# New durations, landing times and priorities for the list planner of a fused attention and expert kernel

## The chip, the core and the metric

The kernel runs on one core of a Trainium2 chip. The metric is the time of one execution in device microseconds, lower is better. The kernel before takes 679.66 us, the median of three runs (678.16 to 679.78).

A core has engines that each work through a queue of instructions in order and wait for each other by semaphores: PE (matrix products into PSUM banks), DVE and ACT (elementwise work), POOL (here mostly the issue of loads) and SP (here the issue of stores).

## The reference

```python
# block attention: a band of +-16 positions, and summaries of blocks of 32
a = softmax(concat(where(mask_l, scale * q @ k.T, -1e9), scale * q @ k_sum.T + log(32)))
x = (a @ concat(v, v_sum)).transpose(0, 2, 1, 3).reshape(3072, 512)
# a dense mixture of experts; P comes from 8 rounds of row and column scaling
P = exp(x @ w_gate - max)
for _ in range(8):
    P /= P.sum(1); P /= P.sum(0); P *= N / E
for e in range(8):
    out += P[:, e:e+1] * (maximum(x @ w1[e], 0) @ w2[e])      # w1[e]: 512 x 1024, w2[e]: 1024 x 512
```

## The kernel before

A first part (to about 164 us of the profiled execution) computes the attention, the gate and expert 0 by ordinary products, and, in a "bridge", the first block of expert 1 beside the eight rounds of scaling. Then comes the repeating part: experts 1 to 7 with both products of each expert done by Winograd's form of Strassen's method (7 block products in place of 8, for more additions). The repeating part is what the change touches.

Each expert `e` is cut into three blocks of columns `j`, and each block into two duos `u` (functions `duo` and `plan_duo`) for the first product and four pairs `c` (functions `pair` and `plan_pair`) for the second.

- A **duo** has two sides, K = 0 and 1. Each side has the PE products `p1` to `p7`, each of two 512 column matmuls (line 990). Between them stand the ACT copies `seed` (line 1091), `c5` (line 1099), `c2` (line 1106), the ACT relus `r11` and `r21` (line 217), and the DVE additions with relu `c12` and `c22` (line 940). `p6` needs `seed`, `p3` needs `c5`, `p7` needs `c2`, `p4` needs `c22`. There is one buffer each for `c5` and for `c2`, so the `c5` copy of one side waits until `c22` of the side before has read the buffer. After both sides come four DVE additions of 1024 columns, `s1` to `s4` (lines 934 and 937).
- From block 2 of expert 1 on, the `p1` of both sides are themselves done by the method: seven single 256 column matmuls `m1` to `m7` (line 1040) with ACT copies `sd` and `c5s` and the DVE additions `j1` (before `m3` and `m7`) and `j2` (before `m4`), which are two of the uses of line 937. There are 38 such split duos among 42.
- A **pair** has the products `q1` to `q7`, each of four 256 column matmuls (line 996), into two banks x and y. ACT makes `c1` and `v6`, DVE makes `v5` (needed by `q6`) and then four accumulations `y0` to `y3` into the output (line 1215). In the last block the pairs c = 1 and 3 use other banks and end in `z0` to `z4`, `x0` and `x1` instead. In expert 1, ACT also scales the output (`scale_a`, `scale_b`, line 1163).
- Beside these, DVE forms the sums of the next expert's weights: `w1_sum` (256 columns), `w2_sum` (1024 columns, four per expert, the first called T1 here) and `wa_sum` (128 columns). POOL issues the loads: `load_w1` (two of 128 KB) and `load_w2` (one of 1 MB).

PSUM has two banks each for the tags ab, g, x and y. A `p1` or `p5` opens an ab bank and so waits until the last user of the old one (`r11` or `c12`) is done.

The order of all this on each engine is not written by hand. `Plan.order` (line 60) is a list planner that runs while the kernel is built: it keeps a clock for each engine, takes for each engine the unit that can start first (within 0.02 us, the one of lowest priority number), lets it last the duration that the code gives (`us`, line 1274), and adds small lags from engine to engine. The instructions are emitted in the order in which they are taken, so every engine's queue is fixed at build time; durations and priorities decide nothing else. Priorities of the repeating part come from the table `PR` (line 1410) plus a base that grows by 100 per duo. For a load the planner assumes an issue time, 0.8 us, a landing time (the fourth argument of `load`) and 0.4 us; units that need the loaded weights start after that.

Of the kernel before, what the change touches and what calls it, by code (L numbers as in the profile page):

```python
# [140 lines left out]
def kernel(  # L141
# [12 lines left out]
    B, H, S, D = q.shape  # L154
# [765 lines left out]
    if True:  # L920
# [232 lines left out]
        def pair(e, j, c, spare=False, tail=False, c1_at=None):  # L1153
# [111 lines left out]
            def x1():  # L1265
# [5 lines left out]
            return {f.__name__: f for f in (scale_a, scale_b, q1, c1, q5, v5, q6, v6, q2, q7, q3, q4, y0, y1, y2, y3, fin, ahead,  # L1271
                                            z3, z2, z0, z4, x0, x1)}

        us = dict(m=0.1092, p=0.4316, q=0.4368, seed=0.49, c5=0.49, c2=0.49, r=0.49, c12=0.607, c22=0.607, s=0.6,
                  c1=0.275, v6=0.275, v5=0.34, y=0.665, half=0.275, join=0.34, w1=0.205, w2=0.6, wa=0.14, x=0.6,
                  xa=0.2, sc=0.62, part=0.34)
        LAGS = {"ACT": 0.06, "DVE": 0.04}

        def put(eng, cost, fn, deps, prio, opens=(), uses=()):
# [121 lines left out]
        for u in course:  # L1401
# [6 lines left out]
        plan.more({"x": 2, "y": 2, "c1": 1, "m5": 1})  # L1408

        PR = {  # L1410
# [8 lines left out]
        }  # L1419
        QO = dict(q1=0, c1=.1, q5=.2, v5=.3, q6=.4, v6=.5, q2=.6, q4=.7, q7=.8, q3=.9)  # L1420
        duos = [(e, j, u) for e in range(1, E) for j in range(NJ) for u in range(2)]
        pairs = {}

        def weights(e, i, deps):
            load(("w1", e, i), lambda: load_w1(e, i), 0.85, 1.3, deps)

        def w_sums(e, i, prio, old=()):
            for n in range(4):
# [26 lines left out]
        def plan_pair(e, j, c, prio):  # L1455
            last_block = e == E - 1 and j == NJ - 1
            spare = last_block and c % 2 == 1
            c1_at = None
            if spare:
                c1_at = lambda: fast.tile([128, 512], FP32, tag=("c2", "c5")[c // 2], name="c1t", bufs=1)[:, 0:DH]  # L1460
            f, d = pair(e, j, c, spare, last_block, c1_at), {}
            src = [made[e, j, 0], made[e, j, 1]]

            def of(*names):
                return [x[n] for x in src for n in names]

            def op(name, eng, cost, deps, opens=(), uses=(), p=None):
                d[name] = put(eng, cost, f[name], [d[y] if isinstance(y, str) else y for y in deps],
                              prio + (QO[name] if p is None else p), opens=opens, uses=uses)

            bx, by = (Buffer(t) for t in (("ab", "g") if spare else ("x", "y")))
            k1 = Buffer("c1")
            c1s = [] if spare else [k1]
            m = us["q"]
            op("q1", "PE", m, of("r110", "r111") + [U["w2", e]] + ([src[1]["c121"], src[1]["r211"]] if spare else []),
               [bx, by])
            op("c1", "ACT", us["c1"], ["q1"] + ([src[1]["c121"], src[1]["c221"]] if spare else []), c1s, [bx])
            op("q5", "PE", m, ["q1", W2[e, 0]] + of("s1"), (), [bx])
            op("v5", "DVE", us["v5"], ["q5", "c1"], (), [bx, by] + c1s)
            op("q6", "PE", m, ["v5", W2[e, 1]] + of("s2"), (), [by])  # L1480
            op("v6", "ACT", us["v6"], ["q6"], (), [by])
            op("q2", "PE", m, ["c1"] + of("r210", "r211"), (), [bx])
            op("q4", "PE", m, ["v5", W2[e, 3]] + of("c220", "c221"), (), [bx])
            op("q7", "PE", m, ["v6", W2[e, 2]] + of("s3"), (), [by])
            op("q3", "PE", m, ["v6"] + of("s4"), (), [by])
            old = []
            if e == 1:
                op("scale_b", "ACT", us["sc"], [], p=PR["sc"])
                op("scale_a", "ACT", us["sc"], [], p=PR["sc"])
                old = ["scale_a", "scale_b"]  # L1490
            if spare:
                op("ahead", "POOL", 0.75, [pairs[e - 1, j, c][y] for y in ("y1", "y2")], p=0)
                op("z3", "ACT", us["half"], ["q3"], (), [by], p=1)
                op("z2", "DVE", us["v5"], ["q7", "ahead"], (), [by], p=1)
                op("z0", "DVE", us["v5"], ["z2"], (), [by], p=1.1)
                op("z4", "POOL", 0.75, ["z3"], p=1)
                op("x0", "DVE", us["v5"], ["q2", "z4"], (), [bx], p=2)
                op("x1", "DVE", us["v5"], ["q4", "z0"], (), [bx], p=2.1)
            else:
                op("y0", "DVE", us["v5"], ["q2"] + old[:1], (), [bx], p=PR["yd"])  # L1500
                op("y1", "DVE", us["v5"], ["q4"] + old[1:], (), [bx], p=PR["yd"] + .1)
                op("y2", "DVE", us["v5"], ["q7"] + old[1:], (), [by], p=PR["yd"] + 2)
                op("y3", "DVE", us["v5"], ["q3", "y0"] + old[:1], (), [by], p=PR["yd"] + 2.1)
                if e == E - 1:
                    op("fin", "POOL" if last_block else "DVE", 0.75 if last_block else us["part"], ["y1", "y2"],
                       p=PR["yd"] + 1)
            pairs[e, j, c] = d

        def feed(n):
            base = 10000.0 + 100.0 * n  # L1510
            if n < len(duos):
                e, j, u = duos[n]
                k = 2 * j + u
                if n == 2:
                    for m in range(4):
                        X[2, m] = put("DVE", us["x"], lambda m=m: x_sum(2, m), [X.get((2, m - 1))], base + 30 + 15 * m)
                    xa_sums(2, base + 100)
                split = None
                if (e, j) >= (1, 2):
                    split = [U["wa", e, u, m] for m in range(4)] + [XA[j, m] for m in range(4)]  # L1520
                free = pair_users(*duos[n - 4][:2]) if n >= 4 else []

                def prio(name):
                    if name in ("s1", "s3", "s2", "s4"):
                        return base + PR["S"] + 0.1 * ("s1", "s3", "s2", "s4").index(name)
                    return base + PR[{"p10": "m1", "p11": "m4"}.get(name, name)]

                made[e, j, u] = plan_duo(e, j, u, prio, split, [made[duos[n - 1]]["p51"]], free,
                                         {(2 * u + h, m): WT[e, 2 * u + h, m] for h in range(2) for m in range(4)},
                                         [X[j, m] for m in range(4)])  # L1530
                if n == 3:
                    p1s = ("p10", "p11")
                    for v in range(2):
                        wa_sums(1, v, base + 30 + 10 * v, users(1, 0, v, p1s) + users(1, 1, v, p1s))
                    for i in range(2):
                        xa_sums(i, base + 150 + 100 * i, users(1, i, 0, p1s) + users(1, i, 1, p1s))
                if e + 1 < E:
                    w = base + PR["w"]
                    if k == 2:
                        load(("w2", e + 1), lambda: load_w2(e + 1), 0.9, 5.0, pair_users(e - 1, 2))  # L1540
                        weights(e + 1, 0, users(e - 1, 2, 1))
                    if k == 3:
                        w2_sums(e + 1, (0, 1), w + 20, pair_users(e - 1, 2))
                        w_sums(e + 1, 0, w, users(e - 1, 2, 1))
                    if k == 4:
                        w2_sums(e + 1, (2, 3), w + 20)
                        weights(e + 1, 1, users(e, 2, 0))
                        weights(e + 1, 2, users(e, 2, 0))
                    if k == 5:
                        w_sums(e + 1, 1, w - 100, users(e, 2, 0))  # L1550
                        wa_sums(e + 1, 0, w - 90, users(e - 1, 2, 1))
                        w_sums(e + 1, 2, w, users(e, 2, 0))
                        weights(e + 1, 3, users(e, 2, 1))
                        w_sums(e + 1, 3, w + 10, users(e, 2, 1))
                        wa_sums(e + 1, 1, w + 20, users(e, 2, 0))
            m = n - 2
            if m < len(duos):
                e, j = duos[m][:2]
                for c in range(2):
                    plan_pair(e, j, 2 * (m % 2) + c, base + PR[f"q{c}"])  # L1560
# [41 lines left out]
```

## Time and profile before

| | us |
| --- | --- |
| median of three runs | 679.66 |
| the profiled execution's own time | 679.68 |
| its span, first to last instruction | 677.7 |
| PE busy | 664.1 |
| DVE busy | 573.5 |
| ACT busy | 420.8 |
| POOL busy | 133.4 |

A row of the timeline gives the start, the duration, the engine, the line, the operation, the tiles (out, then in), the shape and the count of merged instructions, and in brackets the idle time before it and what ended it. A matmul's recorded duration is longer than the time until the next one starts, since they are pipelined; the distance between two starts is what counts for PE. The same holds, less so, for DVE and ACT. A row of stretches gives, after the stretch, the busy time and the number of instructions of each engine, the granted PE clock (1.00 is full), and the use of the DMA engines. Where it is asked for one line only, it counts that line's instructions.

### The profile page before, as it was taken

To read this page: it belongs to the slowest core of one execution; us is meant where nothing else is said; L and a number is where in the kernel's file an instruction comes from. 1 tells how busy PE (TensorE), PEld (TensorE's weight loads), DVE (VectorE), ACT (ScalarE), POOL (GpSimd) and SP (SyncE) were. 2 spreads that over 40 slices of the span, in tenths; PEclk is the share of its full clock that TensorE was granted. 3 is DMA by queue.
4 is the path that set the end of the run, shared out by engine and by line. 5 is a ranking of instruction groups with operands and counts; after the bars stand their busy time and mean duration, and the time that the engine had idled before them with its cause. 6 is when DMAs were issued, how large, how long until landed. Compare 5 with 4: busy or idle time off the path is not lost.

```text
span 677.7 us, 13610 instructions
## 1 busy us (share of the span) xinstructions
PE 664.1 (98%) x5191; PEld 446.7 (66%) x5191; DVE 573.5 (85%) x1447; ACT 420.8 (62%) x858; POOL 133.4 (20%) x179
## 2 busy tenths in 40 slices
PE   8999999999899999999999999999999999999996
PEld 4666655555466676676776766767667667676675
DVE  7889998677789789887988888978988798888795
ACT  6777775566795655665656656565566565665642
POOL 8699404222011010201010010101020101000001
PEclk9999999999899999999999999999999999999999
DMA  9999939401313041310531051304131053101215
GB/s 164 183 149 146 141 72 93 70 1 24 55 17 32 1 66 14 38 11 3 77 32 17 1 78 13 36 1 67 13 36 13 5 75 32 17 1 45 81 63 186
DMA packets 124032, 36.74 MB, mean 54 GB/s; under 512 B 110144, under 2 KB 121152, under 8 KB 123968
## 3 DMA queue, kind: packets, MB, share of 16 engines
q0 software_dynamic: 104128, 25.93, 40.7%
q1 hardware_dynamic: 18880, 9.22, 6.2%
q8 instruction: 40, 0.66, 0.4%
q10 hardware_dynamic: 960, 0.74, 0.3%
q14 instruction: 24, 0.20, 0.1%
HBM read 52.45 MB, written 6.29 MB: 87 GB/s over the span
## 4 chain that ended last, share of the span: by engine, by line
PE 70%; DVE 23%; issue 2%; DMA 2%; ACT 2%; DVEq 0%; ACTq 0%
PE px L996 16%; PE pab L990 12%; PE pg L990 12%; PE py L996 10%; DVE out_acc L1215 6%; PE yps L236 5%; PE hps L226 5%; PE pab L1040 3%; DVE hf L940 3%; DVE hf L934 3%; DVE ws L934 2%; DVE pab L937 1%; DMA w<-in_moe_w_dram 1%; DVE xs L552 1%; DVE hf L937 1%
## 5 line engine op out<-in xcount | busy, mean ns | idle before, releaser
L996 PEld LDWEIGHTS <-hf 128*128 128x128 f16 x2352 | 230.1, 98 | 86.2 <-issue 3.4
L996 PE MATMUL px<-w,hf 128*128 128x256 f16 x656 | 97.9, 273 | 0.0
L996 PE MATMUL px<-ws,hf 128*128 128x256 f16 x656 | 96.1, 274 | 0.0
L996 PE MATMUL py<-w,hf 128*128 128x256 f16 x656 | 93.4, 272 | 0.7 <-DVE out_acc L1215 0.4
L217 ACT ACTIVATE hf<-pab 128x512 f16<-128x512 f32 x84 | 50.2, 599 | 68.2 <-PE pab L990 50.4
L940 DVE CUSTOM_DVE_ANT_0 hf<-pg,c 128x512 f16<-128x512 f32 x84 | 57.6, 686 | 33.7 <-ACT c L1099 30.2
L934 DVE TENSOR_TENSOR hf<-hf 128x1024 f16<-128x1024 f16 x126 | 85.7, 681 | 0.4 <-ACT hf L217 0.3
L202 POOL DMA_DIRECT2D w<-in_moe_w_dram x56 | 41.7, 755 | 215.6 <-PE pg L990 180.5
L1215 DVE SCALAR_TENSOR_TENSOR out_acc<-py,P_sb,out_acc 128x256 f32<-128x256 f32 x164 | 75.2, 474 | 2.7 <-PE py L996 2.6
L1215 DVE SCALAR_TENSOR_TENSOR out_acc<-px,P_sb,out_acc 128x256 f32<-128x256 f32 x164 | 74.4, 474 | 2.1 <-PE px L996 2.1
L940 DVE CUSTOM_DVE_ANT_0 hf<-pab,c 128x512 f16<-128x512 f32 x84 | 57.7, 686 | 21.5 <-PE pab L990 17.7
L990 PEld LDWEIGHTS <-w 128*128 128x128 f16 x520 | 50.8, 98 | 33.2 <-issue 3.6
L1099 ACT COPY c<-pab 128x512 f32<-128x512 f32 x84 | 49.2, 586 | 37.2 <-DVE hf L940 19.6
L1091 ACT COPY pg<-pab 128x512 f32<-128x512 f32 x84 | 48.0, 573 | 33.2 <-PE pab L1040 33.0
L990 PEld LDWEIGHTS <-ws 128*128 128x128 f16 x504 | 49.1, 98 | 28.0 <-issue 7.1
L217 ACT ACTIVATE hf<-pg 128x512 f16<-128x512 f32 x84 | 50.6, 602 | 14.8 <-PE pg L990 12.5
L990 PE MATMUL pab<-xT,w 128*128 128x512 f16 x184 | 54.8, 382 | 0.0
L990 PE MATMUL pg<-xTs,w 128*128 128x512 f16 x168 | 49.9, 378 | 2.9 <-DVE hf L940 2.9
L990 PE MATMUL pab<-xT,ws 128*128 128x512 f16 x168 | 50.0, 379 | 0.6
L990 PE MATMUL pg<-xT,w 128*128 128x512 f16 x168 | 50.4, 382 | 0.0
L1106 ACT COPY c<-pg 128x512 f32<-128x512 f32 x84 | 49.4, 588 | 1.6 <-PE pg L990 1.5
L990 PE MATMUL pg<-xTs,ws 128*128 128x512 f16 x168 | 49.7, 378 | 0.0
(168 smaller groups left out, 1094.7 us busy)
## 6 DMA issues: line engine op xcount, KB each, us to landing
w<-in_moe_w_dram POOLq DMA_DIRECT2D x8, 1024.0 KB, 9.0
w<-in_moe_w_dram POOLq DMA_DIRECT2D x56, 128.0 KB, 3.6
out_dram<-out_acc SPq DMA_DIRECT2D x20, 256.0 KB, 2.1
vx<-in_v_dram POOLq DMA_DIRECT2D x16, 192.0 KB, 6.0
qst<-in_q_dram POOLq DMA_DIRECT2D x31, 96.0 KB, 5.5
kst<-in_k_dram POOLq DMA_DIRECT2D x24, 96.0 KB, 5.4
w<-in_moe_w_dram POOLq DMA_DIRECT2D x2, 512.0 KB, 8.7
Ve<-vx SPq DMA_DIRECT2D x48, 10.2 KB, 4.3
```

The costliest lines, as they stand in the source:

```text
L202: nc.gpsimd.dma_start(out=t[:, :, h, :], in_=moe_w1[e].rearrange("(dk p) f -> p dk f", p=128)[:, :, f:f + 128])
L217: nc.scalar.activation(out=out, in_=in_, func=AF.Relu, bias=0.0, scale=1.0)
L226: nc.tensor.matmul(hp[:, 0:n], lhsT=w1s[e][:, dk, 128 * f:128 * (f + 1)], rhs=xT[:, dk, t0:t0 + n], start=(dk == 0), stop=(dk == KD - 1))
L236: nc.tensor.matmul(yp[:], lhsT=h[:, f, c * 128:(c + 1) * 128], rhs=w2s[e][:, f, :], start=(f == 0), stop=(f == KF - 1))
L934: nc.vector.tensor_tensor(out=out, in0=in0, in1=in1, op=ALU.subtract)
L940: nc.vector._custom_dve(TENSOR_ADD_SAT, out=out, in0=in0, in1=in1, s0=FLT_MAX, s1=0.0)
L990: nc.tensor.matmul(bank[:], lhsT=w[:, dk, :], rhs=x[:, dk, :], start=start and dk == 0, stop=dk == KH - 1, skip_group_check=True)
L996: nc.tensor.matmul(bank, lhsT=a(f)[:, 128 * c:128 * (c + 1)], rhs=w[:, f, :], start=start and f == 0, stop=f == FH - 1, skip_group_check=True)
L1091: nc.scalar.copy(out=B["g" + K][:], in_=B["a" + K][:])
L1099: nc.scalar.copy(out=B["c5" + K][:], in_=B["b" + K][:])
L1106: nc.scalar.copy(out=B["c2" + K][:], in_=B["g" + K][:])
L1215: nc.vector.scalar_tensor_tensor(out=acc, in0=at(src), scalar=P_sb[:, t, e:e + 1], in1=acc, op0=ALU.mult, op1=ALU.add)
```

## The change

Numbers of the planner are changed, and with them the order in which the units come out. No unit is added or removed.

```diff
-        us = dict(m=0.1092, p=0.4316, q=0.4368, seed=0.49, c5=0.49, c2=0.49, r=0.49, c12=0.607, c22=0.607, s=0.6,
-                  c1=0.275, v6=0.275, v5=0.34, y=0.665, half=0.275, join=0.34, w1=0.205, w2=0.6, wa=0.14, x=0.6,
-                  xa=0.2, sc=0.62, part=0.34)
+        us = dict(m=0.1092, p=0.4316, q=0.4368, seed=0.55, c5=0.5, c2=0.49, r=0.49, c12=0.607, c22=0.607, s=0.6,
+                  c1=0.34, v6=0.28, v5=0.35, y=0.395, half=0.275, join=0.335, w1=0.205, w2=0.6, wa=0.14, x=0.6,
+                  xa=0.2, sc=0.63, part=0.34)
...
-            "m1": -147.7, "sd": -402.0, "m5": -279.9, "c5s": 449.5, "m2": -40.2, "m6": -290.7,
...
+            "m1": -361.0, "sd": -416.8, "m5": -89.0, "c5s": 512.2, "m2": -93.3, "m6": -289.5,
...
-            load(("w1", e, i), lambda: load_w1(e, i), 0.85, 1.3, deps)
+            load(("w1", e, i), lambda: load_w1(e, i), 0.85, 2.5, deps)
...
-                op("y0", "DVE", us["v5"], ["q2"] + old[:1], (), [bx], p=PR["yd"])
-                op("y1", "DVE", us["v5"], ["q4"] + old[1:], (), [bx], p=PR["yd"] + .1)
-                op("y2", "DVE", us["v5"], ["q7"] + old[1:], (), [by], p=PR["yd"] + 2)
-                op("y3", "DVE", us["v5"], ["q3", "y0"] + old[:1], (), [by], p=PR["yd"] + 2.1)
+                op("y0", "DVE", us["y"], ["q2"] + old[:1], (), [bx], p=PR["yd"])
+                op("y1", "DVE", us["y"], ["q4"] + old[1:], (), [bx], p=PR["yd"] + .1)
+                op("y2", "DVE", us["y"], ["q7"] + old[1:], (), [by], p=PR["yd"] + 2)
+                op("y3", "DVE", us["y"], ["q3", "y0"] + old[:1], (), [by], p=PR["yd"] + 2.1)
...
-                        load(("w2", e + 1), lambda: load_w2(e + 1), 0.9, 5.0, pair_users(e - 1, 2))
+                        load(("w2", e + 1), lambda: load_w2(e + 1), 0.9, 8.0, pair_users(e - 1, 2))
```

So the accumulations `y0` to `y3`, and `z0`, `z2`, `x0`, `x1` of the last block in the same way, are planned with 0.395 us in place of 0.34; `seed`, `c5`, `c1`, `v6` and `v5` last a little longer in the plan; a `load_w2` lands 3.0 us later in the plan and a `load_w1` 1.2 us later; and all 43 numbers of `PR` but one are new.

More of the change, by code (lines that the diff above doesn't have):

```diff
@@ L1493, in plan_pair @@
                 op("z3", "ACT", us["half"], ["q3"], (), [by], p=1)
-                op("z2", "DVE", us["v5"], ["q7", "ahead"], (), [by], p=1)
-                op("z0", "DVE", us["v5"], ["z2"], (), [by], p=1.1)
+                op("z2", "DVE", us["y"], ["q7", "ahead"], (), [by], p=1)
+                op("z0", "DVE", us["y"], ["z2"], (), [by], p=1.1)
                 op("z4", "POOL", 0.75, ["z3"], p=1)
-                op("x0", "DVE", us["v5"], ["q2", "z4"], (), [bx], p=2)
-                op("x1", "DVE", us["v5"], ["q4", "z0"], (), [bx], p=2.1)
-            else:
-                op("y0", "DVE", us["v5"], ["q2"] + old[:1], (), [bx], p=PR["yd"])
-                op("y1", "DVE", us["v5"], ["q4"] + old[1:], (), [bx], p=PR["yd"] + .1)
-                op("y2", "DVE", us["v5"], ["q7"] + old[1:], (), [by], p=PR["yd"] + 2)
-                op("y3", "DVE", us["v5"], ["q3", "y0"] + old[:1], (), [by], p=PR["yd"] + 2.1)
+                op("x0", "DVE", us["y"], ["q2", "z4"], (), [bx], p=2)
+                op("x1", "DVE", us["y"], ["q4", "z0"], (), [bx], p=2.1)
+            else:
+                op("y0", "DVE", us["y"], ["q2"] + old[:1], (), [bx], p=PR["yd"])
+                op("y1", "DVE", us["y"], ["q4"] + old[1:], (), [bx], p=PR["yd"] + .1)
+                op("y2", "DVE", us["y"], ["q7"] + old[1:], (), [by], p=PR["yd"] + 2)
+                op("y3", "DVE", us["y"], ["q3", "y0"] + old[:1], (), [by], p=PR["yd"] + 2.1)
                 if e == E - 1:
```

14 rows, old and new, of the table PR are left out of this document.

## Prediction

> **What bounds the kernel now.** I read the page first, then the waits, then PE's timeline by the distance between starts, since the recorded length of a matmul hides small waits.
>
> ```profile
> span 677.7 us, 13610 instructions
> ...
> w<-in_moe_w_dram POOLq DMA_DIRECT2D x8, 1024.0 KB, 9.0
> ```
>
> ```profile
> 164.10 1.03 PE L990 MATMUL pab<-xT,w 128*128 128x512 f16 x4
> 164.96 1.04 PE L996 MATMUL px<-w,hf 128*128 128x256 f16 x8
> 165.83 1.03 PE L990 MATMUL pg<-xTs,ws 128*128 128x512 f16 x4
> 166.70 1.03 PE L990 MATMUL pab<-xT,w 128*128 128x512 f16 x4
> 167.56 0.59 PE L990 MATMUL pg<-xT,w 128*128 128x512 f16 x2
> ```
>
> Eight matmuls of 512 columns start within 165.83 to 167.56: 0.216 us each. Eight of 256 take 164.96 to 165.83: 0.109. So a `p` costs 0.43 and a `q` 0.44 when nothing waits. Here PE runs without a gap. Counting matmuls in two stretches, by lines 990, 996 and 1040, shows how much it loses elsewhere:
>
> ```profile
> 182.00:657.97 475.97, 253.73 (x934) 90.86 (x933) 1.00 0.23 32
> 407.22:480.69 73.47, 39.31 (x145) 14.02 (x145) 1.00 0.25 30
> ```
>
> ```profile
> 182.00:657.97 475.97, 294.59 (x2174) 212.13 (x2173) 1.00 0.23 32
> 407.22:480.69 73.47, 45.59 (x338) 32.77 (x336) 1.00 0.25 30
> ```
>
> ```profile
> 182.00:657.97 475.97, 62.20 (x266) 25.94 (x266) 1.00 0.23 32
> 407.22:480.69 73.47, 9.95 (x42) 4.09 (x42) 1.00 0.25 30
> ```
>
> Long stretch: 934 x 0.216 + 2440 x 0.109 = 467.7 of 475.97, a loss of 8.3 us. One expert (407.22 to 480.69, the same point of the next one): 144 x 0.216 + 378 x 0.109 = 72.3 of 73.5, a loss of 1.15 (145 and 338 reach over the edge). Experts 2 to 6 repeat it: 5.8 of the 8.3; the other 2.5 lie where expert 1 passes into 2, and in expert 7. So PE's work bounds the repeating part, and an order can win back only such losses, and one larger one:
>
> ```profile
> 171.47 0.60 PE L996 MATMUL px<-w,hf 128*128 128x256 f16 x4
> 174.95 0.59 PE L990 MATMUL pg<-xTs,w 128*128 128x512 f16 x2 [2.88 <-DVE hf L940]
> ```
>
> ```profile
> 169.75 0.43 DVE L937 TENSOR_TENSOR py<-px,c 128x256 f32<-128x256 f32 x1 [0.62 <-ACT c L1187]
> 173.60 0.69 DVE L934 TENSOR_TENSOR ws<-w 128x1024 f16<-128x1024 f16 x1 [3.42 <-DMA w<-in_moe_w_dram]
> 174.21 0.68 DVE L940 CUSTOM_DVE_ANT_0 hf<-pg,c 128x512 f16<-128x512 f32 x1
> ```
>
> ```profile
> 164.56 0.94 POOL L213 DMA_DIRECT2D w<-in_moe_w_dram  x1 [1.41 <-PE yps L236]
> ```
>
> ```profile
> 175.00:180.00 5.00, 4.99 (x19) 2.45 (x19) 4.57 (x11) 3.95 (x7) 0.00 (x0) 0.66 0.00 0
> ```
>
> The 1 MB load of expert 2's `w2` is issued at 164.56 and lands 9.0 later, at 173.6. DVE has come to T1 of those weights at 170.2 and stands 3.42; `c22` is behind it in the queue, and PE's `p4` waits for `c22`. PE's four matmuls end their slot at 171.47 + 0.44 = 171.91, so it idles 3.04. Then the granted clock is 0.66 over the next 5.0 us: another 5.0 x 0.34 = 1.7. Together 4.7 us. (The Trainium skill, page "TensorE: Matmul & The Clock Gate", Part 1, says that PE goes to half clock after an idle window of about 3.4 us that runs freely; the trace agrees that some 3 us suffice.)
>
> **The change, part by part.** No instruction is added or removed, and up to the bridge the queues stand as before; only places in the order change.
>
> *The landing times.* The plan before expects `w2` 0.8 + 5.0 + 0.4 = 6.2 after its issue unit, the new one 9.2; the row says 9.0 from issue. In the new DVE order T1 stands behind `v5`, `c22`, `y0`, `c12` and the second `v5`, all of expert 1, block 1. I walk through that place from the 164.10 of `p1`.
>
> ```profile
> 164.78 1.07 ACT L1091 COPY pg<-pab 128x512 f32<-128x512 f32 x2
> 165.77 0.39 ACT L1187 COPY c<-px 128x256 f32<-128x256 f32 x1
> 166.03 0.74 ACT L1163 ACTIVATE out_acc<-out_acc,P_sb 128x512 f32<-128x512 f32 x1
> ```
>
> ACT's new order after the two seeds (end 165.85) is scale, `c2`, `c1`, `r11`, `r11`, scale, `c5`: `c2` can start at 166.6, and 0.6 + 0.4 + 0.6 + 0.6 + 0.7 + 0.6 put the end of `c5` at 170.1 (copies and relus of 512 columns at 0.6, the longest reading of the row of seeds). `c22` (0.68) then ends at 170.85, and `p4`, 15 products after 164.10 and so due at 170.6, loses 0.3. The second `v5` follows `q5`, the 17th product: DVE reaches T1 at about 172.4 and waits 1.2 for 173.6 instead of 3.4. T1 takes until 174.2, `c12` until 174.9; this frees the bank of the 24th product, a `p1` due at about 174.5: 0.4. With 0.1 each at `p3` and `p7`, behind ACT, PE loses 0.9. Bounds: 0.5, when ACT's ops take their shorter distance; 2.0, when `c22`, one op later than `c12`, also holds `p4`, and the first of these waits adds up. No wait comes near 3 us, so I take the clock as full. Gain 4.7 - 0.9 = 3.8 (2.7 to 4.2). The loads themselves are issued in the same order on POOL, and in the repeating experts no row has DVE waiting for a load: there the later landing costs nothing, hidden by a block of PE work.
>
> *The durations.* What is lost in a repeating expert shows in two kinds of places.
>
> ```profile
> 406.46 0.68 DVE L940 CUSTOM_DVE_ANT_0 hf<-pg,c 128x512 f16<-128x512 f32 x1
> ...
> 411.46 0.68 DVE L934 TENSOR_TENSOR hf<-hf 128x1024 f16<-128x1024 f16 x1
> 412.06 0.48 DVE L1215 SCALAR_TENSOR_TENSOR out_acc<-px,P_sb,out_acc 128x256 f32<-128x256 f32 x1
> 412.46 0.42 DVE L937 TENSOR_TENSOR pab<-pab,m 128x256 f32<-128x256 f32 x1
> ```
>
> ```profile
> 407.23 0.59 ACT L1099 COPY c<-pab 128x512 f32<-128x512 f32 x1 [0.66 <-DVE hf L940]
> ```
>
> ```profile
> 407.22 0.59 PE L990 MATMUL pg<-xTs,w 128*128 128x512 f16 x2
> 407.86 0.59 PE L990 MATMUL pab<-xT,ws 128*128 128x512 f16 x2
> ```
>
> ```profile
> 412.06 0.60 PE L996 MATMUL px<-w,hf 128*128 128x256 f16 x4
> 412.59 0.60 PE L996 MATMUL px<-ws,hf 128*128 128x256 f16 x4
> ```
>
> First: `c22` ends late on a full DVE (407.14), the `c5` copy waits for its buffer and ends at 407.82, and `p3` starts 0.64 after the product before it instead of 0.43: 0.21 lost, in two of an expert's duos. Second: `q4` starts at 412.59, 0.53 after `q2`, since `y0` on its bank stood behind an `s` until 412.06: 0.1 lost. The distance between starts says why: an `s` holds DVE 0.60 and a `y` 0.40, and the old plan had 0.34 for a `y`. With 48 of them per expert, 48 x 0.06 = 2.9 us of DVE work were not in the plan. The new one has 0.395.
>
> I then counted in both orders how much PE work stands between an op's trigger and the product that needs the op. From `p5` to `p3` (over `c5`) the least is 0.87 before and 1.31 after; it needs 0.16 (a matmul group's 0.59 less its 0.43) + 0.59 + some 0.1 of signals = 0.85 with a free ACT, so the new order has 0.4 to spare and the 2 x 0.21 go. `q3` behind `y2` at 0.87 is gone too. `q4` close behind `y0` goes from 18 places at 1.09 to 11 at 0.98, but with `y0` no longer behind an `s`: 0.16 + 0.48 + 0.1 = 0.74. Against the change: `m7` behind `j1` shrinks from 1.3 (36 of 38 duos) to 0.87 (33 of 38), need 0.16 + 0.42 + 0.1 = 0.68, and `p4` behind `c22` stays at 0.98 with a need of 0.94. Adding DVE's queue op by op over a block with these distances (0.60, 0.40, 0.33), every op of it comes in time, by 0.02 to 0.3. So an expert should lose 0.1 to 0.6 in place of 1.15; I take 0.35, since margins are thin: 5 x 0.8 = 4.0. Bounds for the five: 5.5 and, if new small waits replace the old ones, 0.
>
> For the other 2.5 I take back 0.5: after T1 lands late, DVE still has some 20 ops to catch up in block 1 of expert 1 (eight small weight sums, four `s`, seven `y`), and the products of the next pairs wait for banks. Bounds 2.0 and -1.0.
>
> *The tail.* Before, these are the last product, `z4` and `x1`:
>
> ```profile
> 671.51 0.60 PE L996 MATMUL py<-w,hf 128*128 128x256 f16 x4
> ```
>
> ```profile
> 672.32 0.72 POOL L1259 TENSOR_TENSOR out_acc<-out_acc,y 128x256 f32<-128x256 f32 x1
> ```
>
> ```profile
> 673.86 0.47 DVE L1266 SCALAR_TENSOR_TENSOR out_acc<-pab,P_sb,out_acc 128x256 f32<-128x256 f32 x1
> ```
>
> The last product ends at 672.11 and DVE's last op at 674.33. In the new order the `q3` that leads over ACT and POOL to `x0` is third from last, two products (0.87) earlier, and `y2`, `x0`, `y3` are left in place of five ops. Two ops less at 0.40 would be 0.8; POOL's step holds part of it: 0.6 (0 to 0.9).
>
> *The sum:* 3.8 + 4.0 + 0.5 + 0.6 = 8.9 from the profiled execution's 679.68 (span 677.7 and 2.0 around it), which the median of 679.66 matches: **670.8 us**.
>
> **The rivals.** (a) *Only the large wait goes.* The margins counted above are smaller than what the old order had at `j1`, and the waits of the repeating experts change places without shrinking: 679.7 - 3.8 = 675.9. For it speaks DVE's full stretch around 411; against it the block added up.
>
> (b) *The load's wait takes the place of itself.* T1 still comes before the load, by 1.2; if ACT runs ahead of my walk, DVE stands there longer, `c12` and `c22` behind it hold `p1` and `p4` some 2 to 3, with the clock falling again: only 1 to 2 of the 4.7 are won, 679.7 - 1.5 - 5.1 = 673.1. Against it: `v5`, which stands before T1, cannot run before `q5`, so DVE cannot be there before 171.6.
>
> (c) *Slower: `j1` late in each split duo.* With 0.87 instead of 1.3 in front of `m7`, one `s` (0.60) that gets in ahead of `j1` costs 0.60 - 0.19 = 0.41 each time; 38 split duos make 15.6, and the sum is 679.7 - 8.9 + 15.6 = 686.4. It turns the result slower from 8.9/38 = 0.23 lost per duo on. For it: the distance is shorter in most duos. Against it: `p4` behind `c22` had only 0.04 to spare before and no row of the waits names it there. (The Trainium skill, page "VectorE: DVE Perf Modes", section "The DRAIN you can't avoid", says that the next op does not start until the pipeline has emptied; by that an `s` would hold DVE its full 0.68, the plan would be too short again, and this rival would follow. The trace has starts 0.60 apart.)
>
> (d) *The change does nothing*, since the order comes out alike: excluded, PE's and DVE's queues differ throughout the repeating part.
>
> **How the numbers follow.** Forecast (gain of 6 to 12) 0.65; (a) 0.17; (b) 0.10; (c) 0.05, mostly far below its full price; 0.03 for anything else. Low end: 4.2 + 5.5 + 2.0 + 0.9 = 12.6 gives 667.1. High end: (a) with nothing from the tail, 675.9. What a measurement can tell is 0.3%, 2.0 us. Forecast, (a) and (b) are all faster than that: 0.91 with a little taken off; same 0.04; slower 0.05.
>
> **What would show it.** DVE's wait for the load near 172 at 1 to 1.5 and no clock under 1.00 in 175 to 180 show the first step; a distance between the same points of two experts of 72.4 to 72.9 the second; the last DVE op 1.5 to 2 after the last product the tail. Wrong would be a distance of 73.5 (a), a clock below 1.00 again (b), or `m7` starting late in each duo (c).

## The result, and the profile after

The changed kernel takes 669.1 us, the median of four runs (668.87 to 669.73), against 679.34 us for the kernel before (four runs, 678.16 to 679.78): a ratio of 0.9853, with a 95% interval of 0.9836 to 0.9871. The profiled execution took 669.18 us with a span of 667.5, 10.2 us less than the span before.

The page of the kernel after, its span and its first, third and fourth part: busy times, the load's row and the chain.

```profile
span 667.5 us, 13584 instructions
...
PE 655.8 (98%) x5191; PEld 446.7 (67%) x5191; DVE 577.0 (86%) x1448; ACT 420.5 (63%) x857; POOL 133.6 (20%) x179
...
PE 90%; DVE 7%; DMA 1%; issue 1%; ACT 0%; POOL 0%; POOLq 0%; ACTq 0%; DVEq 0%
...
w<-in_moe_w_dram POOLq DMA_DIRECT2D x8, 1024.0 KB, 9.0
```

The load still takes 9.0 us. What changed is where things stand. The bridge is planned with the same durations, so its order changes too, from 134 us on, but the first product after it starts at 164.07 in place of 164.10. First the place between the two blocks of expert 1, in the timeline of the kernel after: POOL's issue, DVE, then PE, and the row of the stretch that had a clock of 0.66.

```profile
164.54 0.94 POOL L213 DMA_DIRECT2D w<-in_moe_w_dram  x1 [2.28 <-PE yps L236]
```

```profile
171.71 0.43 DVE L937 TENSOR_TENSOR py<-px,c 128x256 f32<-128x256 f32 x1 [0.20 <-PE px L996]
173.62 0.69 DVE L934 TENSOR_TENSOR ws<-w 128x1024 f16<-128x1024 f16 x1 [1.47 <-DMA w<-in_moe_w_dram]
174.23 0.68 DVE L940 CUSTOM_DVE_ANT_0 hf<-pab,c 128x512 f16<-128x512 f32 x1
```

```profile
173.61 0.60 PE L996 MATMUL py<-w,hf 128*128 128x256 f16 x4
174.96 0.59 PE L990 MATMUL pab<-xT,w 128*128 128x512 f16 x2 [0.76 <-DVE hf L940]
```

```profile
175.00:180.00 5.00, 5.00 (x34) 3.24 (x34) 5.00 (x14) 4.32 (x8) 0.00 (x0) 1.00 0.00 0
```

T1 (at 173.62) waits 1.47 instead of 3.42, and what stands behind it is `c12`. The bank that this frees is needed by a `p1`: four matmuls start at 173.61, their slot ends at 174.05, and the next product starts at 174.96, so PE loses 0.91. The clock stays at 1.00.

Second, the repeating experts: the first matmul of an `m7`, and that of the same `m7` one expert later, before and then after.

```profile
400.34 0.27 PE L1040 MATMUL pab<-xT,w 128*128 128x256 f16 x1
...
473.81 0.27 PE L1040 MATMUL pab<-xT,w 128*128 128x256 f16 x1
```

```profile
381.27 0.27 PE L1040 MATMUL pab<-xT,w 128*128 128x256 f16 x1
...
453.62 0.27 PE L1040 MATMUL pab<-xT,w 128*128 128x256 f16 x1
```

73.47 us before, 72.35 after. The sum of the matmuls alone was 72.3 in the prediction: such an expert now runs with hardly a loss. (Of the five periods of experts 2 to 6, four are 72.34 or 72.35 long and one is 72.64, with a wait of 0.24 at 368.) The view of PE's waits, which goes by recorded idle time, has three left from 160 us on, in the kernel after (engine and line, what was waited for, total, times, longest):

```profile
PE pab L990 <- DVE hf L940: 0.8, 1, 0.8
PE px L996 <- ACT c L1187: 0.6, 1, 0.6
PE pg L990 <- DVE hf L940: 0.2, 1, 0.2
```

Shorter waits hide behind the recorded lengths of the matmuls. The distances between starts show three more, of 0.22 to 0.24 us.

Third, the end. The last two products, `z3` on ACT, POOL's two steps (`z4` and `fin`) and DVE's last sum in the kernel after:

```profile
660.79 1.04 PE L996 MATMUL py<-w,hf 128*128 128x256 f16 x8
661.04 0.47 ACT L1247 ACTIVATE y<-pg,P_sb 128x256 f32<-128x256 f32 x1 [1.00 <-PE pg L996]
661.59 0.72 POOL L1259 TENSOR_TENSOR out_acc<-out_acc,y 128x256 f32<-128x256 f32 x1 [4.39 <-ACT y L1247]
...
662.43 0.73 POOL L1236 TENSOR_TENSOR out_acc<-out_acc 128x256 f32<-128x256 f32 x1
662.66 0.48 DVE L1215 SCALAR_TENSOR_TENSOR out_acc<-py,P_sb,out_acc 128x256 f32<-128x256 f32 x1
```

The last product ends at 661.83 and DVE at 663.14, 1.3 later (2.2 before). But the span ends 5.6 after the last product, as it did before (672.11 to 677.7). The tail gave nothing.

The distances between the starts of PE's products, less 0.432 for a `p`, 0.436 for a `q` and 0.109 for an `m`, add up to a loss of 13.3 us before and 3.05 after, from 164 us on. The difference, 10.25, is the whole gain in the span (10.2). Between the blocks of expert 1 (164 to 182) it is 4.9 - 0.9, in experts 2 to 6 (from the first `m1` of expert 2 to that of expert 7) it is 6.2 - 0.5, and the rest is about 0.6 (2.3 - 1.7).

### The profile page after: what moved, and what is told of

The parts are those of the page before. It is cut to its first block, busy times and chain, and to the rows that moved or that the text cites. A ratio compares the mean times of both kernels' runs of the same rounds, so it can differ in the third digit from the quotient of the medians.

```text
span 667.5 us, 13584 instructions
## 1 busy us (share of the span) xinstructions
PE 655.8 (98%) x5191; PEld 446.7 (67%) x5191; DVE 577.0 (86%) x1448; ACT 420.5 (63%) x857; POOL 133.6 (20%) x179
## 4 chain that ended last, share of the span: by engine, by line
PE 90%; DVE 7%; DMA 1%; issue 1%; ACT 0%; POOL 0%; POOLq 0%; ACTq 0%; DVEq 0%
PE px L996 21%; PE pab L990 16%; PE pg L990 16%; PE py L996 16%; PE yps L236 5%; PE hps L226 5%; PE pab L1040 4%; DVE xs L552 1%; DMA vx<-in_v_dram 1%; PE sg L388 1%; PE tkq L354 1%; PE ss L475 1%; PE tx L559 1%; DVE out_acc L1215 0%; DVE hf L940 0%
## 5 line engine op out<-in xcount | busy, mean ns | idle before, releaser
L996 PE MATMUL px<-ws,hf 128*128 128x256 f16 x656 | 98.4, 273 | 0.6 <-ACT c L1187 0.6
L996 PE MATMUL py<-w,hf 128*128 128x256 f16 x656 | 89.1, 273 | 0.0
L1215 DVE SCALAR_TENSOR_TENSOR out_acc<-py,P_sb,out_acc 128x256 f32<-128x256 f32 x164 | 72.2, 476 | 0.7 <-PE py L996 0.7
L1091 ACT COPY pg<-pab 128x512 f32<-128x512 f32 x84 | 48.0, 573 | 16.2 <-PE pab L1040 14.8
L990 PE MATMUL pab<-xTs,ws 128*128 128x512 f16 x168 | 49.8, 379 | 0.0
## 6 DMA issues: line engine op xcount, KB each, us to landing
Ve<-vx SPq DMA_DIRECT2D x48, 10.2 KB, 3.9
```

What stands on the lines that cost most here:

```text
L990: nc.tensor.matmul(bank[:], lhsT=w[:, dk, :], rhs=x[:, dk, :], start=start and dk == 0, stop=dk == KH - 1, skip_group_check=True)
L996: nc.tensor.matmul(bank, lhsT=a(f)[:, 128 * c:128 * (c + 1)], rhs=w[:, f, :], start=start and f == 0, stop=f == FH - 1, skip_group_check=True)
L1091: nc.scalar.copy(out=B["g" + K][:], in_=B["a" + K][:])
L1215: nc.vector.scalar_tensor_tensor(out=acc, in0=at(src), scalar=P_sb[:, t, e:e + 1], in1=acc, op0=ALU.mult, op1=ALU.add)
```

## The experiments

The change has three parts: durations, landing times, priorities. The first question was what each does alone. In the tables and readings below, "period" is the time from an `m7` to the same `m7` one expert later, as above. A ratio is that to runs of the kernel before made beside the run, whose medians were 678.9 to 679.3.

**One landing time.** The kernel before, with only the load of expert 2's `w2` planned 3 us later.

```diff
-  load(("w2", e + 1), lambda: load_w2(e + 1), 0.9, 5.0, pair_users(e - 1, 2))
+  load(("w2", e + 1), lambda: load_w2(e + 1), 0.9, 8.0 if e == 1 else 5.0, pair_users(e - 1, 2))
```

> The kernel before with one number changed: the landing time of expert 2's w2 load alone is planned at 8.0 instead of 5.0. Theory (that one load, met too early by T1 on DVE, costs 3.0 of PE idle and 1.7 of low clock): DVE has no wait for a load near 170, no clock under 1.00 in 175 to 180, 4 to 4.7 us gained, 674.6 to 675.3; the repeating experts keep their 73.5 us each. Rival (the wait only changes place): gain under 2, 677.3 or more.

674.98 us, ratio 0.9943 (0.9924 to 0.9962). The large wait and the low clock are gone and the period stays at 73.49. One number of the plan is worth some 4 us: 3.9 against the 678.9 of the kernel before beside it, and 4.5 in PE's losses.

**The durations alone, and the priorities alone.** The two lines of `us` with the uses of `us["y"]`, and the table `PR`, each put into the kernel before by itself; the landing times stay old.

```diff
-        us = dict(m=0.1092, p=0.4316, q=0.4368, seed=0.49, c5=0.49, c2=0.49, r=0.49, c12=0.607, c22=0.607, s=0.6,
+        us = dict(m=0.1092, p=0.4316, q=0.4368, seed=0.55, c5=0.5, c2=0.49, r=0.49, c12=0.607, c22=0.607, s=0.6,
```

```diff
-            "m1": -147.7, "sd": -402.0, "m5": -279.9, "c5s": 449.5, "m2": -40.2, "m6": -290.7,
+            "m1": -361.0, "sd": -416.8, "m5": -89.0, "c5s": 512.2, "m2": -93.3, "m6": -289.5,
```

> The kernel before with the new durations alone (y planned with its own 0.395); priorities and landing times are the old ones. T1 again stands behind the first v5: about 6 us lost there. Theory (true durations are enough to keep the waits of the repeating experts small, whatever the priorities): 72.4 to 72.8 per expert and 674 to 677 in all. Rival (priorities found for other durations do not fit): 73.5 or more per expert, 680 or more.

> The kernel before with the new priorities alone; durations and landing times are the old ones. T1 stands behind the first v5 as in the run with the old landing times, so about 6 us are lost there. Theory (the repeating experts lose time because 2.9 us of DVE work per expert are missing from the plan): they lose 1 us or more each as before, 679 to 681 in all. Rival (the priorities do it, whatever the durations): 72.3 to 72.5 per expert and 674 to 675 in all.

The durations alone give 673.18 (0.9914, 0.9891 to 0.9937), a little under the expected 674 to 677, although they make the place in expert 1 worse: T1 moves ahead there.

```profile
173.58 0.69 DVE L934 TENSOR_TENSOR ws<-w 128x1024 f16<-128x1024 f16 x1 [5.32 <-DMA w<-in_moe_w_dram]
```

```profile
174.93 1.01 PE L990 MATMUL pg<-xTs,w 128*128 128x512 f16 x2 [4.17 <-DVE hf L940]
```

```profile
175.00:180.00 5.00, 5.00 (x16) 2.24 (x16) 3.59 (x8) 3.37 (x6) 0.00 (x0) 0.50 0.00 0
```

The period, however, falls to 72.34. The priorities alone make the kernel slower: 684.97 (1.0094, 1.0068 to 1.0119), 4 us above the expected 679 to 681, with a period of 75.22 (74.7 to 75.4 over experts 2 to 6). So the new durations take the losses out of the repeating experts under the old priorities, and the new priorities by themselves do not; what they add, the next run shows.

**The old landing times in the kernel after.** Durations and priorities new.

```diff
-            load(("w1", e, i), lambda: load_w1(e, i), 0.85, 2.5, deps)
+            load(("w1", e, i), lambda: load_w1(e, i), 0.85, 1.3, deps)
...
-                        load(("w2", e + 1), lambda: load_w2(e + 1), 0.9, 8.0, pair_users(e - 1, 2))
+                        load(("w2", e + 1), lambda: load_w2(e + 1), 0.9, 5.0, pair_users(e - 1, 2))
```

> The changed kernel with the two landing times set back to 5.0 and 1.3; durations and priorities are the new ones. T1 then stands right behind the first v5 on DVE, so DVE should stand from about 167.8 to 173.6 and p4, due at 170.5, should start near 174.9: 4.3 of idle and 1.7 of low clock in place of 0.9. Theory: 669.1 + 5.1 = 674.2, with the repeating experts as in the changed kernel (72.3 to 72.4 us each). Rival (the landing times do nothing, the new priorities alone keep T1 away): 669.1.

683.92 us, ratio 1.007 (1.0048 to 1.0092): slower than before, and 9.7 us more than expected. The large wait is back as expected, but the period is also 73.91 (73.1 to 74.8 over experts 2 to 6). DVE's waits for loads from 160 us on, in this kernel:

```profile
DVE ws L937 <- DMA w<-in_moe_w_dram: 7.0, 5, 2.0
...
DVE ws L934 <- DMA w<-in_moe_w_dram: 5.9, 1, 5.9
```

The first row is new: in five experts a sum of `w1` waits for its 128 KB load, which lands 3.6 us after its issue:

```profile
w<-in_moe_w_dram POOLq DMA_DIRECT2D x56, 128.0 KB, 3.6
```

The old plan counted 0.8 + 1.3 + 0.4 = 2.5 for it. With the old priorities this error never showed; the new priorities take the sums early enough that it does. The priorities-only run has the same two rows (7.0 and 5.9).

**The old priorities in the kernel after.** Durations and landing times new, the table old.

```diff
-            "m1": -361.0, "sd": -416.8, "m5": -89.0, "c5s": 512.2, "m2": -93.3, "m6": -289.5,
+            "m1": -147.7, "sd": -402.0, "m5": -279.9, "c5s": 449.5, "m2": -40.2, "m6": -290.7,
```

> The kernel after with the old priorities: the new durations and the new landing times are kept. Theory: the new durations alone take the losses out of experts 2 to 6 (the run with durations only came to 673.2 us with some 6.8 us lost between expert 1's blocks), and the new landing time moves the first w2 sum behind `c12`, so that this 6.8 falls to about 0.9; the new priorities give nothing of their own. 673.2 - 5.9 = 667.3 us, between 666.5 and 668.5, and each of experts 2 to 6 loses less than 0.1 us on PE. Rival: the later landing times move the loads and the 128 KB sums so that only priorities found with them hide them; then the repeating experts lose 0.3 us or more each and the time is 669.1 us or above.

668.5 us, five runs (0.9844, 0.9827 to 0.9861), with a period of 72.35 and 2.45 us of PE lost from 164 us on. The theory holds: the new priorities give nothing that can be measured against the changed kernel's 0.9853 (0.9836 to 0.9871). (No run has the old durations with the new priorities and the new landing times, so it is not shown whether priorities alone can take out the losses once the loads are planned right.)

**Which duration.** The kernel before with only `y` planned at 0.395 us, and its counterpart with all new durations but that one.

```diff
-                  c1=0.275, v6=0.275, v5=0.34, y=0.665, half=0.275, join=0.34, w1=0.205, w2=0.6, wa=0.14, x=0.6,
+                  c1=0.275, v6=0.275, v5=0.34, y=0.395, half=0.275, join=0.34, w1=0.205, w2=0.6, wa=0.14, x=0.6,
...
-                op("y0", "DVE", us["v5"], ["q2"] + old[:1], (), [bx], p=PR["yd"])
+                op("y0", "DVE", us["y"], ["q2"] + old[:1], (), [bx], p=PR["yd"])
```

> The kernel before with one duration changed: the last sums `y`, `x` and `z` are planned at 0.395 us each instead of the 0.34 of `v5` (`us["y"]` takes their place). All other durations, the landing times and the priorities are the old ones. Theory: DVE is short of time in each half block because four `y` sums were planned 0.055 us too short, and these late sums were what made `c12` and `j1` late; then experts 2 to 6 lose about nothing, and with the transition as in the kernel before (the first w2 sum still behind two `v5`, some 4.9 us lost) the time is 673.8 us (673 to 675). Rival: the longer durations on ACT (`seed` 0.55, `c1` 0.34) are what removes the losses: then experts 2 to 6 lose 1.15 us each as before and the time is 679 us.

> The kernel before with all the new durations except that of `y`, which stays at 0.34 us; landing times and priorities are the old ones. It is the counterpart of the run with `y` alone (672.5 us, 0.4 us lost in experts 2 to 6 against 5.3 before). Theory: `y`'s duration alone makes the plan of the repeating experts fit, so without it experts 2 to 6 lose about 1.1 us each again; the first w2 sum stands behind one `v5` only, as in the run with all durations, so some 6.8 us are lost between expert 1's blocks: 679.3 - 13.3 + 5.3 + 6.8 + 1.5 (rest) = 679.6 us, between 678 and 681. Rival: the other durations (`seed`, `c1`) remove the losses as well; then experts 2 to 6 lose under 0.5 us in all and the time is 673 to 675 us.

With `y` alone 672.47 us (0.9895, 0.9875 to 0.9915), without it 680.3 us (1.0013, 1.0004 to 1.0022). The same `m7` again, with `y` alone and then with all but `y`:

```profile
385.51 0.27 PE L1040 MATMUL pab<-xT,w 128*128 128x256 f16 x1
...
457.86 0.27 PE L1040 MATMUL pab<-xT,w 128*128 128x256 f16 x1
```

```profile
375.74 0.27 PE L1040 MATMUL pab<-xT,w 128*128 128x256 f16 x1
...
449.21 0.27 PE L1040 MATMUL pab<-xT,w 128*128 128x256 f16 x1
```

72.35 and 73.47. The duration of `y` is sufficient and necessary; `seed` and `c1` do not count here. (Only 0.34 and 0.395 were tried: that the loss goes because the number fits the 0.40 of the trace, and would not go with a larger one, is argued and not shown.) In the run without it the small waits are at other products than before (a `q3` 0.19 late, five times per expert), but they come to the same 1.1 in the period: the plan lacks the same 2.9 us of DVE's work per expert, and where it comes out depends on the order. (The run with `y` alone came out 1.3 below the expected 673.8: the sum had left out that the losses outside experts 2 to 6 and the place in expert 1 shrink too, from 2.3 to 0.9.)

**A late `j1`.** Three unused sums on DVE, 128 x 128, right ahead of each `j1`, in the kernel after and in the kernel before. They add work and change no result.

```diff
             def j1():
+                for n in range(3):
+                    sub(spent[:], zeros[:], zeros[:])
                 plus(B["a0"][:, 256:512], B["a1"][:, 0:256], B["m5"][:])
```

> The kernel after with three more sums on DVE (128 x 128 bf16, some 0.14 us each, their output never used) right ahead of each `j1`, so that in every split duo `j1` comes some 0.42 us later. Theory (the prediction's third rival, its price): `j1` ends 0.19 us before its consumer, so 0.23 us of PE is lost in each of 38 duos, 8.7 us in all: 677.8 us (675 to 682). Rival: DVE runs ahead by more than the order shows, or catches up, and the sums cost under 2 us: 669 to 671 us.

> The kernel before with the same three sums ahead of each `j1`, beside the run with them in the kernel after. Theory: before, `j1` had 1.3 us to its consumer, so 0.42 us does not reach PE there; only the three waits for late sums that each expert has already can grow, each by at most 0.42 us: 679.3 us up to 684 us, and an increase smaller than the one in the kernel after. Rival: what counts is DVE's added work (38 times 0.42 us), not where it stands: both kernels get longer by the same amount within 2 us.

688.35 us after (1.0128, 1.0106 to 1.015) and 703.2 us before (1.0348, 1.0327 to 1.0369): 19 and 24 us more, and both above what was expected (at most 682 and 684). The three sums in the kernel before with them, its next `j1`, the `m7` behind it:

```profile
409.85 0.74 DVE L934 TENSOR_TENSOR spent<-zeros 128x128 bf16<-128x128 bf16 x3
...
410.51 0.42 DVE L937 TENSOR_TENSOR pab<-pab,m 128x256 f32<-128x256 f32 x1
...
410.99 0.27 PE L1040 MATMUL pab<-xT,w 128*128 128x256 f16 x1 [0.27 <-DVE pab L937]
```

They hold DVE for 0.66 (409.85 to 410.51), not the estimated 0.42. They start at 409.85, 410.11 and 410.37: all three write the same buffer, and in the trace the second and the third each wait for the one before. `j1`, which does not, starts 0.14 after the third, as estimated. The `m7` starts 0.06 after the recorded end of `j1`; that is the least distance (0.05 or 0.06 in all 38 duos of both runs). Without the sums, it is this in the kernel after, and this before (the `m7` there is the row at 400.34 above):

```profile
405.19 0.43 DVE L937 TENSOR_TENSOR pab<-pab,m 128x256 f32<-128x256 f32 x1
...
405.82 0.27 PE L1040 MATMUL pab<-xT,w 128*128 128x256 f16 x1
```

```profile
399.64 0.42 DVE L937 TENSOR_TENSOR pab<-pab,m 128x256 f32<-128x256 f32 x1
```

405.82 - 405.62 = 0.20 after, so some 0.15 to spare (in most duos the distance is 0.17 or 0.23); 400.34 - 400.06 = 0.28 before, so some 0.23. Each duo then pays 0.66 less the margin: 0.51 x 38 = 19.4 after, where 19.2 was measured. Before it would be 0.43 x 38 = 16; the other 8 are further waits (a `q4` behind `v5` 0.33 late, an `m4` 0.24), because that order had no room elsewhere either. Both of the numbers behind the second expectation fall: the margin before was never 1.3, and under this load the older order is the more fragile one.

**The store on SP's queue.** One wait of PE in the kernel after, 0.6 behind a `c1` copy, was not foreseen. The timeline of the kernel after around it:

```profile
655.59 0.72 POOL L1259 TENSOR_TENSOR out_acc<-out_acc,y 128x256 f32<-128x256 f32 x1 [52.91 <-ACT y L1247]
...
656.31 0.47 DVE L1215 SCALAR_TENSOR_TENSOR out_acc<-pab,P_sb,out_acc 128x256 f32<-128x256 f32 x1
656.47 0.73 POOL L1236 TENSOR_TENSOR out_acc<-out_acc 128x256 f32<-128x256 f32 x1 [0.16 <-DVE out_acc L1215]
...
656.86 0.36 ACTq L1219 DMA_DIRECT2D out_dram<-out_acc  x1
...
657.31 0.37 ACT L1187 COPY c<-px 128x256 f32<-128x256 f32 x1 [1.81 <-POOL out_acc L1236]
...
657.74 0.60 PE L996 MATMUL px<-ws,hf 128*128 128x256 f16 x4 [0.56 <-ACT c L1187]
```

The store of `x0` is issued on ACT's queue, at 656.86, right after the sum `x0` on DVE (656.31 to 656.78); `z4` on POOL, which it needs too, had ended at 656.31. (The bracket of the copy names POOL's line 1236, but that step ends at 657.20, after the store was issued.) The copy that stands behind the store on ACT starts only at 657.31, and PE's next product (four matmuls had started at 656.58) at 657.74, 0.72 late. The edit moves the store to SP's queue, in the kernel after and in the one with the old priorities.

```diff
             def x0():
                 add_to(ta, 0, 0)
-                store(ta, eng=nc.scalar)
+                store(ta)
```

> The kernel after, with the one store of the last block that was issued on ACT's queue (`x0`'s) issued on SP's queue. Theory: the 0.72 us that PE stands still at 656.6 is the `c1` copy of pair c2 waiting on ACT behind this store's own wait for `z4`; with the store on SP the copy starts when its product ends, the stall goes, and the time falls by 0.6 to 0.7 us to about 668.4 us. Rival: the copy is late for another reason (ACT's own work, or DVE behind it), or the time comes back in the tail because the store starts later: 669.1 us as before, the stall still there or the last store landing later.

> Both edits together: the old priorities with the new durations and landing times, and `x0`'s store on SP's queue. Theory: if both stand, about 666.7 us (667.3 with the old priorities, less 0.6 if the old priorities' last block has the same wait behind the store), and never above the run with the old priorities alone by more than 0.2 us. Rival: the last block's order with the old priorities has no such wait, and the edit changes nothing: 667.3 us.

On the kernel after: 667.98 us (0.9835, 0.9818 to 0.9852). The wait is gone from the trace and PE loses 2.29 in place of 3.05 us, so the theory holds, except that the store waited for `x0` itself and not for `z4`. With the old priorities: 669.55 us (0.9856, 0.984 to 0.9872), where the rival stands: that order had no such wait (2.40 lost against 2.45), and the edit does nothing. That it reads 1 us more than without the edit is not the edit's doing. Of the 1.68 us between the two profiled executions (669.78 and 668.10), 0.75 lie in the first part, which is the same in both kernels and ended at 164.32 with the edit and at 163.57 without, and 1.0 lies outside the span (2.8 us against 1.8). Over all kernels here the first part ended between 163.4 and 165.1, and in the kernel after with its store on SP it ended 0.6 earlier than without. Differences of 1 us between medians are within that; the 0.76 of that edit rests on the trace.

**Smaller last stores.** On top of that store on SP, in the kernel after, the 256 KB stores behind the last two sums are split in two, so that 128 KB stand behind each.

```diff
             def y0():
                 add_to(ta, 0, 0)
+                if tail and e == E - 1:
+                    store(ta, slice(0, DH))
...
                 if e == E - 1:
-                    store(ta)
+                    store(ta, slice(DH, DM) if tail else slice(0, DM))
...
             def fin():
+                if tail:
+                    store(tb, slice(DH, DM))
                 between(out_acc[:, tb, 0:DH], out_acc[:, tb, DH:DM], out_acc[:, tb, 0:DH])
-                store(tb)
+                store(tb, slice(0, DH) if tail else slice(0, DM))
```

> The kernel after with `x0`'s store on SP's queue (668.0 us), and besides this in the last block the 256 KB stores that follow `fin` and `y3` split in two: the half row that is ready earlier is stored at once, and only 128 KB stand behind the last sum. Theory: with a 256 KB store last, the end came 4.30 us after the last sum; with a 128 KB store last (old priorities) it came 3.37 us after it. So the time falls by 0.9 us to 667.1 us. Rival: the end is not set by the last store's size (the time from the last product to the end was 5.5 to 5.7 us in nearly every run, whatever the order): 668.0 us.

668.26 us (0.9834, 0.9814 to 0.9853), no difference from 667.98 that can be measured. In the profiled executions the end came 5.12 after the last product in place of 5.60: half of the expected 0.9, and too little to show. The trace has the other half. Four stores now stand on SP's queue at the end, which issues one after another, 0.4 to 0.5 apart, so the last one is issued 1.06 after the last sum (662.40 to 663.46); its 128 KB then land in 1.8. None of the variants is shown to be faster than the changed kernel; the interval of the lowest median, 667.98, overlaps with its own.

The medians side by side:

| durations | landing | priorities | us | period |
| --- | --- | --- | --- | --- |
| old | old | old | 679.3 | 73.47 |
| old | `w2` of expert 2 new | old | 675.0 | 73.49 |
| only `y` new | old | old | 672.5 | 72.35 |
| all but `y` new | old | old | 680.3 | 73.47 |
| new | old | old | 673.2 | 72.34 |
| old | old | new | 685.0 | 75.22 |
| new | old | new | 683.9 | 73.91 |
| new | new | old | 668.5 | 72.35 |
| new | new | new | 669.1 | 72.35 |

## Why the prediction was right, and where it was not

The forecast was 670.8 us for a measured 669.1; the sum had 8.9 us, and 10.2 came.

- **The landing times**: right in mechanism and size. The gain was 3.8 by the walk and 4.0 by the trace; T1's wait was put at 1.2 and is 1.47, PE's loss was put at 0.9 and is 0.9, the clock stayed full. The 0.9 lies almost all at the `p1` behind `c12`, where the walk had spread it over four products. The run with one landing time, some 4 us faster, shows that this mechanism stands by itself. What the prediction said of the repeating experts, that the later landing costs nothing there, holds in the changed kernel; the reason behind it was too wide. It read from the kernel before that no sum waits for a load there, and that is a property of the old priorities: with the new ones the old landing times cost 14.8 us, of which some 8 lie in experts 2 to 6 (370.0 us for the five against 362.0).
- **The durations**: the mechanism was right, the term was mis-sized. "I take 0.35, since margins are thin" should have been next to nothing: 72.35 is left of 73.47, and the five experts gave 5.7 instead of 4.0, a little over the upper bound of 5.5. The 48 `y` sums per expert, named as the cause, are the cause by themselves, as the two runs with and without them show.
- **The other 2.5 us**: 0.5 was taken back, some 0.6 came, in spite of a new wait of 0.72 behind a store on ACT's queue. That wait was missed because PE, ACT and DVE were followed op by op and the DMA issues on ACT's queue were not.
- **The tail**: failed. 0.6 was expected and nothing came. DVE did finish earlier than forecast (1.3 instead of 1.5 to 2 after the last product), but `fin` moved behind `z4` on POOL, and last now are stores of 256 KB, where it was one of 128 KB. Before, the last store was issued 0.03 after the last sum and landed 2.1 later; after, it is issued 0.5 after it, behind the store of `fin` on SP's queue, and lands 2.6 later. These 1.0 us eat the 0.9 that DVE gained. The step counted ops and left out what has to be issued and to land behind them.
- **Rival (c)**: did not come, and its price was tested. The margin of 0.19 worked out for the changed kernel is about what the trace has (0.15), and lateness beyond it is paid almost in full in each duo. Its premise is refuted: distance in the order, counted from an op's trigger to its consumer, is no slack when the engine's queue is full in between. The old order's 1.3 at `j1` was 0.23 in the trace, so the shorter distances of the new order (0.15) cost hardly any slack, which also takes away the ground of rival (a). Rival (b) is refuted by the clock of 1.00.

## What to carry to other kernels

Where a list planner fixes the order, compare its durations with the distance between starts in the trace, count by count: one op planned 0.055 us too short, 48 times per expert, cost 1.1 us per expert on the engine that bounds the kernel, while new priorities gave nothing measurable, and with wrong landing times made the kernel slower than before. Read the slack of a wait from the trace (end of the producer to start of the consumer, less the least distance seen) and not from positions in the order. Follow every queue at the place that moves, the DMA issues on compute engines and the size and place of the last store among them.

## What the hardware showed

The lowered clock was half of the full one in every run that had it, behind shorter and longer idle times alike. The 0.66 of the kernel before over 175 to 180 is a mean: it set in at 176.4, 1.5 us after PE had started again, and lasted 3.4 us. Three stretches of the kernel before:

```profile
174.00:176.40 2.40, 1.44 (x6) 0.58 (x6) 2.40 (x7) 1.46 (x3) 0.00 (x0) 1.00 0.20 20
176.45:179.80 3.35, 3.35 (x14) 1.76 (x13) 2.92 (x8) 2.51 (x5) 0.00 (x0) 0.50 0.00 0
179.85:182.00 2.15, 2.15 (x18) 1.54 (x17) 1.67 (x5) 1.55 (x3) 0.00 (x0) 1.00 0.00 0
```

With the durations alone, behind a recorded idle time of 4.17 us, it set in at 173.2, while PE still stood, and lasted 6.8 us; so it fills the 5 us from 175 on, which read 0.50. One stretch of that run:

```profile
173.20:179.95 6.75, 5.02 (x16) 2.31 (x16) 4.95 (x9) 3.46 (x6) 0.00 (x0) 0.50 0.12 11
```

What it costs is half of the time that PE works in it. The shortest recorded idle time behind which the clock fell is 2.77 us (`y` alone), the longest that left it full is 1.98 (the priorities alone, at 337.45, with a clock of 1.00 over 334 to 340); where it falls in between is not known. (The Trainium skill, page "TensorE: Matmul & The Clock Gate", Part 1, gives an idle window of some 3.4 us; here less than that was enough, and the measurement decides.)

The short price of a small DVE op held here only where it did not wait. The 128 x 128 f16 sums in the kernel after stand 0.13 from the next start (176.42 to 176.55 in DVE's timeline); the unused sums ahead of `j1`, which wait for each other, stood 0.26 apart.
